# From the seventh query block on, the local scores and the preceding block's products with V become one task of the ordering list

## The chip, the cores and the metric

The kernel runs on one core of a Trainium2 chip. The metric is the device time of one launch in microseconds (us). Five engines work side by side, each through its own instructions in a fixed order: PE (TensorE, matmuls; its weight loads are listed as PEld), DVE (VectorE), ACT (ScalarE), POOL (GpSimd) and SP (SyncE, which here only issues DMAs). An engine that waits for a semaphore holds up everything behind it in its own list.

## The reference

The inputs q, k and v have 8 batches, 8 heads, 576 positions and 64 elements per head. The attention has two parts that are added; the result goes through a feed-forward network (FFN) with a residual.

```python
q_d = q.reshape(B, H, Sd, factor, D).mean(axis=3)      # factor 4: 144 pooled positions; k_d, v_d alike
out_up = np.repeat(sm_attn(q_d, k_d, v_d), factor, axis=2)
mask = np.abs(pos[:, None] - pos[None, :]) < factor     # a band of 7 positions
scores = np.where(mask, scale * q @ k.T, -1e9)
out_local = softmax(scores) @ v
x = (out_up + out_local)                                # 4608 tokens of 512
xn = (x - mean) / sqrt(var + 1e-6) * g_ln
out = x + relu(xn @ w_ch1) @ w_ch2                      # 512 -> 2048 -> 512
```

## The kernel before

**The FFN** fills most of PE's time. The 4608 tokens are 18 chunks of 256. For each chunk there are 8 pairs of hidden slices (2 x 128 of 2048 columns). An operand is split into a high and a low part, and each product is made of three matmuls (low by high, high by low, high by high). "Up" (`up`, L1048) makes `h` in PSUM, 12 matmuls of 128x256 for each slice; ACT makes `hh` from it (L1055) and DVE the rest `hl` (L1059); "down" (`down`, L1071) adds 6 matmuls of 128x512 for each slice into the two `acc` tiles of the chunk, which stay in PSUM for the chunk's whole life. The first two chunks run interleaved while the weights arrive. A weight slab `s` is loaded by two DMAs of SP, put together by ACT (L359) and DVE (L367, L370) as `cva`, and split by ACT (L378) and DVE (L383) into `hi` and `lo`. There are 32 slabs: `1_f` and `2_f` for f from 0 to 15.

**The local attention** has 40 query blocks (`local(i)`, i from 0 to 39, five for each batch, each of two rows of 58 queries against 64 keys). For the blocks from 7 on SP loads q and k in 128-byte pieces (`qr`, `kr`, L478, 16 DMAs for a block) and v (`vwin`, L496, 4 DMAs); DVE transposes q and k (`lqt`, `lkt`, L535); PE makes the scores `ls` with 32 matmuls of 64x64 (`scores_by_block`, L587); DVE adds the mask (L593), takes the largest (L598) and from block 12 on subtracts it (L603); ACT makes the exponentials `la` (L613; before block 12 eight small ones, L617, with a scaling on DVE, L600); PE transposes them (`lt`, L622); ACT copies them out (`at`, L629); PE multiplies them with V (`times_v`, `lv`, 32 matmuls of 64x65, L643); DVE takes inverses (`lr`, L649, L650) and divides (`xl`, L659; or ACT with four small instructions, L662); SP moves the rows to the token tiles (`x<-xl`, L708, L714). Two matmuls of 64x64 tiles stand in different quarters of the PE array and run at the same time, four of them side by side.

**The pooled attention** works on 16 half batches with two head pairs each: `raw` loads, POOL sums (L765, L766), PE transposes `gq` (L791), ACT copies (`qbdg`, L800, `ktg`, L804), PE scores `gs` (L818), DVE the largest `gmx` (L822), ACT exponentials `ag` (L831), PE transposes `gt` (L837), ACT `agt` (L847), PE products with V `gv` (L854), DVE `od`. Then each tile of 128 tokens is added up by POOL (L948), normed by DVE (`st`, `mv`, `xn`) and turned by PE (`px`, L975).

**What sets the order.** All of this is put on record as tasks of a list (`Plan.add`): an engine, an estimated duration, the tasks it depends on, a due time, and the rooms that it takes and gives back. Rooms are "u" (88 tiles of 2 KB in SBUF), "stg" (2 staging tiles) and "a" (the 8 PSUM tiles). `Plan.order` then pulls due times forward through the dependencies and puts one task after another: on the engine that can go on first, the ready task that is due first and whose rooms are free. The emitted instruction order of every engine is that order, and on the chip each engine follows it whatever the estimates were worth. A block's due time is `window_at(i)`: 25.2 units of the plan's own time from one block to the next, with blocks 5 and 6 put 50 units early. The scores of a block are due 6 units before it, its `lt` 3 before, its product with V 1 before. The loads of q and k are due 14 units before.

Of the kernel before, what the change touches and what calls it, by code (L numbers as in the profile page):

```python
# [22 lines left out]
class Plan:  # L23
# [14 lines left out]
    def add(self, eng, dur, fn, deps=(), due=0.0, take=(), give=(), lag=None, ahead=1e9, alt=None, kb=0):  # L38

        opts = {eng: (dur, fn, 0.0)}  # L40
        if alt is not None:
            opts[alt[0]] = alt[1:]
        t = SimpleNamespace(
            n=len(self.tasks), opts=opts, dur=dur, deps=[d for d in deps if d is not None],
            due=due, take=take, give=give, lag=lag, ahead=ahead, open=0.0, waits=0, eng=None, fn=None, kb=kb,
        )
        self.tasks.append(t)
        return t
# [91 lines left out]
def attention_then_ffn(  # L140
# [13 lines left out]
    B, H, S, D = q.shape  # L154
# [8 lines left out]
    NWIN = 5  # L163
# [7 lines left out]
    NPAIR = H // 2  # L171
    NU, NSTG = 88, 2
    NPE, NPB = 7, 1
    NVW = 4
# [2 lines left out]
    NU -= sum(SEP.values())  # L177
    SHIFTED = (0, 1, 2, 3)
    LATE = 12
    SCALE = 1.0 / float(D) ** 0.5  # L180
    POOLED_SCALE = SCALE / (FACTOR * FACTOR)
    out_f = out.rearrange("b s e -> (b s) e")
# [111 lines left out]
    def window_at(i):  # L294
        if NWIN <= i < NWIN + NEARLY:
            return w_base + i * w_gap - EARLY
        return w_base + i * w_gap if i >= NWIN else norm_at(0) - B0W - B0W_GAP * (2 - i)
# [7 lines left out]
    AHEAD = 45  # L305
# [4 lines left out]
    plan = Plan({"u": NU, "stg": NSTG, "a": 8, **SEP}, {"a": 2, "u": U_SPARE})  # L310
# [8 lines left out]
    U, A, STG = (("u", 1),), (("a", 1),), (("stg", 1),)  # L319
    DMA, LAT, W_AHEAD, W_LAG = 0.5, 2.5, 40, 1.5  # L320

    def act(n, sbuf=False):
        return (0.155 if sbuf else 0.14) + n / 1430.0

    def dve(n):
        return 0.06 + n / 950.0
# [132 lines left out]
    last_local = SimpleNamespace(v=[None] * NVW, ls=None)  # L459
# [3 lines left out]

    def local(i):
        b, w = divmod(i, NWIN)
        due = window_at(i)
        add = plan.add
        x = SimpleNamespace(r={}, p={}, raw={})
        vwin = vwins[i % NVW]
# [37 lines left out]
        turned = []  # L507
        by_pe = i < NPE
        own = b < NPB
        for src, nm in () if own else ((q, "q"), (k, "k")):  # L510
            if by_pe:
# [10 lines left out]
                def turn_out(nm=nm):  # L522
# [4 lines left out]
                t = add("SP", 1.33, lambda src=src, nm=nm: load_rows(src, nm), (), due - 12.0, take=U,  # L527
                        lag=LAT, kb=360, ahead=AHEAD)
                t = add("PE", 0.43, turn, (t,), due - 8.0, take=A, give=U)
# [15 lines left out]
        if own:  # L545
# [2 lines left out]
                if half in {int(window_start(w, par) + 64 > FACTOR * OWN_G[0][1]) for par in range(2)}:  # L548
                    turned += own_done[b, half]
            turned.append(last_local.ls)  # L550
        vt = add("SP", 2.65 if own else 2.65, load_v, (last_local.v[i % NVW],), due - 8.0, lag=LAT, kb=360, ahead=AHEAD)

        def scores_by_pair():

# [37 lines left out]
        def masked(n):  # L592
            nc.vector.tensor_add(x.ps[n], x.ps[n], mask.unsqueeze(1).broadcast_to([P, NPAIR, 64]))  # L593
# [37 lines left out]
        def times_v():  # L631


            x.pv = [
                psa(f"lv{i}_{n}")[:, : NPAIR * (D + 1)].rearrange("p (h e) -> p h e", h=NPAIR)
                for n in range(2)
            ]
            for pr in range(NPAIR):
                for n in range(2):
                    js = slice(64 * n, 64 * n + 64)  # L640
                    for m in range(2):
                        hs = slice(64 * m, 64 * m + 64)
                        nc.tensor.matmul(  # L643
                            x.pv[n][hs, pr], lhsT=x.at[js, pr, hs], rhs=vwin[js, m, pr], start=True, stop=True
                        )

        def inverse(h2):
            r = work.tile([P, NPAIR], F32, tag="lr", bufs=8, name=f"lr{i}_{h2}")
            nc.vector.tensor_scalar_add(r, x.pv[h2][:, :, D], 1e-9)  # L649
            nc.vector.reciprocal(r, r)  # L650
            x.r[h2] = r

        def divided(h2, eng):
# [7 lines left out]
            for pr in range(NPAIR):  # L661
                nc.scalar.activation(xl[:, pr], pv[:, pr, :D], AF.Copy, scale=r[:, pr : pr + 1])  # L662

        by_dve = i in SHIFTED or i >= LATE
        t = add("PE", 0.75, scores_by_pair if by_pe else scores_by_block, turned, due - 6.0,
                take=(("a", 2),), give=() if own and w not in (2, NWIN - 1) else (("u", 2 * NPAIR if own else 2),))
        if own:
            last_local.ls = t
        if not by_pe:
            t = add("DVE", dve(256), lambda: masked(0), (t,), due - 5.0)  # L670
            t = add("DVE", dve(256), lambda: masked(1), (t,), due - 5.0)
        t = add("DVE", 2 * dve(256) + (2 * dve(256) if by_dve else 0.15), largest_by_pair, (t,), due - 5.0)
        t = add("ACT", 2 * act(256) if by_dve else 1.6, exps_by_pair, (t,), due - 5.0, take=U, give=(("a", 2),))
        t = add("PE", 0.43, turn_a, (t,), due - 3.0, take=A, give=U)
        at = add("ACT", act(512), turn_a_out, (t,), due - 3.0, take=U, give=A)
        last_local.v[i % NVW] = tv = add("PE", 0.7, times_v, (at, vt), due - 1.0, take=(("a", 2),), give=U)
        outs = []
        for h2 in range(2):
            t = add("DVE", 0.28, lambda h2=h2: inverse(h2), (tv,), due)
# [5 lines left out]
        for par in range(2):  # L685
            s0 = NQ * (2 * w + par)
            n = min(NQ, S - s0)
            t, r0 = b * S + s0, s0 - window_start(w, par)
            while n:
                m = min(n, P - t % P)  # L690
                moves.append((t // P, t % P, r0, m, par))
                t, r0, n = t + m, r0 + m, n - m
# [478 lines left out]
```

## Time and profile before

| | |
|---|---|
| median of 3 runs | 1054.72 us (1051.92 to 1056.3) |
| profiled execution: its own time, which is its span | 1051.3 us |
| mean granted TensorE clock | 0.995 |
| PE busy | 1034.3 us, 98% |
| DVE / ACT / POOL busy | 514.0 / 309.8 / 251.0 us |
| 1152 + 1152 + 1152 matmuls of L1048, 3 x 576 of L1071 | busy 193.6 + 185.2 + 185.0 and 237.2 + 227.4 + 225.2 us, overlapping each other |
| `ls` by blocks, 1056 matmuls of 64x64 (L587) | busy 22.9 us |
| `lv`, 1280 matmuls of 64x65 (L643) | busy 28.2 us |

How to read it: matmuls are pipelined, so the records of one overlap those of the next, and what a group costs PE is read from the start of one record to the start of the next. In the timeline the first column is the start in us from the span's start, the second the time from the first start to the last end of the merged records; a bracket gives idle time just before and what ended it. In the windows, each engine has its busy time and the number of instructions, then come the granted PE clock (1.00 is full), the DMA share and GB/s.

### The profile page before, as it was taken

How to read it: one execution, taken by the hardware profiler on the slowest of the kernel's cores; microseconds unless marked ns; L12 is line 12 of the kernel's file. 1: busy time of each engine (PE TensorE's matmuls, PEld its weight loads, DVE VectorE, ACT ScalarE, POOL GpSimd, SP SyncE). 2: the span in 40 equal slices, each digit the busy share in tenths (PEclk: the TensorE clock that was granted, in tenths of full speed). 3: DMA queues.
4: the chain of work that ended last, by engine and by line, in shares of the span. 5: the costliest groups of instructions: out<-in, count | busy, mean ns of one | idle time of the engine just before them, and what ended most of it. 6: DMA issues, size and time to landing. Idle time of an engine off the chain costs nothing.

```text
span 1051.3 us, 24104 instructions
## 1 busy us (share of the span) xinstructions
PE 1034.3 (98%) x9450; PEld 928.9 (88%) x9450; DVE 514.0 (49%) x1301; ACT 309.8 (29%) x846; POOL 251.0 (24%) x272
## 2 busy tenths in 40 slices
PE   9999899999999999999999999999999999999998
PEld 8887798988899989989898989899989899888997
DVE  7799976343444435444434443544434444534211
ACT  6676533232212222221323222222221222221110
POOL 4213552214014320231404150141401300000000
PEclk9999999999999999999999999999999999999999
DMA  7897474434344534343434443253442443301000
GB/s 177 251 283 210 136 176 95 114 64 114 61 101 91 133 75 110 62 124 56 91 94 96 104 97 99 47 134 67 114 87 69 92 88 65 80 11 52 7 21 21
DMA packets 283702, 104.38 MB, mean 99 GB/s; under 512 B 229789, under 2 KB 270493, under 8 KB 283589
## 3 DMA queue, kind: packets, MB, share of 16 engines
q1 hardware_dynamic: 283589, 102.84, 40.8%
q8 instruction: 75, 1.23, 0.5%
q14 instruction: 38, 0.31, 0.1%
HBM read 82.58 MB, written 11.80 MB: 90 GB/s over the span
## 4 chain that ended last, share of the span: by engine, by line
PE 83%; DVE 6%; DMA 5%; SPq 2%; issue 1%; POOL 1%; ACT 1%; ACTq 0%; DVEq 0%; POOLq 0%
PE h L1048 34%; PE acc L1071 33%; PE gv L854 3%; DMA s<-in_moe_w_ch_dram 2%; PE gs L818 2%; PE lv L643 2%; PE ls L587 2%; DVE cva L370 2%; PE lt L622 1%; PE px L975 1%; PE gt L837 1%; DVE lo L383 1%; SPq L714 1%; DMA x<-xl 1%; DVE cva L367 1%
## 5 line engine op out<-in xcount | busy, mean ns | idle before, releaser
L1071 PE MATMUL acc<-hi,hl 128*128 128x512 f32 x576 | 237.2, 412 | 0.6 <-DVE hl L1059 0.5
L1071 PE MATMUL acc<-lo,hh 128*128 128x512 f32 x576 | 227.4, 395 | 0.0
L1071 PE MATMUL acc<-hi,hh 128*128 128x512 f32 x576 | 225.2, 391 | 0.0
L1059 DVE SCALAR_TENSOR_TENSOR hl<-h,hh 128x512 fp32r<-128x512 f32 x144 | 98.9, 687 | 250.7 <-ACT hh L1055 222.0
L1055 ACT ACTIVATE hh<-h 128x512 fp32r<-128x512 f32 x144 | 86.2, 599 | 430.3 <-PE h L1048 363.5
L1048 PE MATMUL h<-xh,lo 128*128 128x256 f32 x1152 | 193.6, 291 | 0.2 <-DVE lo L383 0.2
L1048 PE MATMUL h<-xh,hi 128*128 128x256 f32 x1152 | 185.2, 283 | 0.0
L1048 PE MATMUL h<-xlo,hi 128*128 128x256 f32 x1152 | 185.0, 283 | 0.0
L1048 PEld LDWEIGHTS h<-xh,lo 128*128 128x128 f32 x1152 | 169.0, 190 | 17.4 <-DVE lo L383 0.4
L1048 PEld LDWEIGHTS h<-xlo,hi 128*128 128x128 f32 x1152 | 158.9, 192 | 0.0
L1048 PEld LDWEIGHTS h<-xh,hi 128*128 128x128 f32 x1152 | 158.6, 191 | 0.0
L948 POOL TENSOR_TENSOR x<-x,up 128x512 f32<-128x512 f32 x32 | 41.2, 1287 | 386.3 <-DMA x<-xl 208.1
L1071 PEld LDWEIGHTS acc<-hi,hh 128*128 128x128 f32 x576 | 108.5, 188 | 25.0
L1071 PEld LDWEIGHTS acc<-hi,hl 128*128 128x128 f32 x576 | 109.2, 190 | 16.9 <-DVE hl L1059 1.2
L1071 PEld LDWEIGHTS acc<-lo,hh 128*128 128x128 f32 x576 | 109.5, 190 | 12.7 <-DVE lo L383 0.3
L982 ACT ACTIVATE xh<-px,gain 128x128 fp32r<-128x128 f32 x144 | 43.7, 372 | 72.7 <-PE px L975 42.4
L992 DVE SCALAR_TENSOR_TENSOR xlo<-px,gain,xh 128x128 fp32r<-128x128 f32 x144 | 43.1, 345 | 39.1 <-ACT xh L982 38.6
L1079 DVE SCALAR_TENSOR_TENSOR x<-acc,x 128x512 f32<-128x512 f32 x36 | 24.7, 689 | 39.8 <-PE acc L1071 39.8
L831 ACT ACTIVATE ag<-gs,gmx 96x144 f32<-96x144 f32 x96 | 29.0, 374 | 41.9 <-DVE gmx L823 34.4
L370 DVE SCALAR_TENSOR_TENSOR cva<-s,cva 128x256 int32<-128x256 int32 x64 | 40.0, 665 | 1.1
L854 PEld LDWEIGHTS gv<-vd,agt 72*72 72x72 f32 x512 | 37.1, 145 | 1.2
L854 PE MATMUL gv<-vd,agt 72*72 72x65 f32 x512 | 37.9, 228 | 0.0
(196 smaller groups left out, 1106.9 us busy)
## 6 DMA issues: line engine op xcount, KB each, us to landing
s<-in_moe_w_ch_dram SPq DMA_DIRECT2D x64, 256.0 KB
vwin<-in_v_dram SPq DMA_DIRECT2D x160, 64.0 KB
out_dram<-x SPq DMA_DIRECT2D x36, 256.0 KB
qr<-in_q_dram SPq DMA_DIRECT2D x264, 32.0 KB
kr<-in_k_dram SPq DMA_DIRECT2D x264, 32.0 KB
up<-ud SPq DMA_DIRECT2D x28, 256.0 KB
x<-xl SPq DMA_DIRECT2D x74, 42.0 KB
ud<-od SPq DMA_DIRECT2D x32, 72.0 KB
```

Source lines behind the costliest of these rows:

```text
L370: nc.vector.scalar_tensor_tensor(out=a, in0=x.raw[i].rearrange("p (n two) -> p n two", two=2)[:, :, 0], scalar=29, in1=a, op0=ALU.logical_ ...
L587: nc.tensor.matmul(x.ps[par][64 * h2 : 64 * h2 + 64, pr], lhsT=x.qt[hs, 2 * pr + h2], rhs=x.kt[hs, 2 * pr + h2], start=True, stop=True,)
L831: nc.scalar.activation(y.a[:, c], y.ps[:, c], AF.Exp, scale=POOLED_SCALE, bias=y.mx[:, c : c + 1])
L854: nc.tensor.matmul(y.pv[:, qh, h2], lhsT=y.at[kh][:, h2, qh * GH : (qh + 1) * GH], rhs=vd[:, kh, 2 * pr + h2], start=kh == 0, stop=kh == 1,)
L948: nc.gpsimd.tensor_add(xt[n], xt[n], x.up)
L982: nc.scalar.activation(xh[c][i][:, k, j * P : (j + 1) * P], pxt[n][:, kc], AF.Copy, scale=gain[:, kc : kc + 1])
L992: nc.vector.scalar_tensor_tensor(out=xlo[c][i][:, k, ts], in0=pxt[n][:, kc], scalar=gain[:, kc : kc + 1], in1=xh[c][i][:, k, ts].bitcast(F ...
L1048: nc.tensor.matmul(ph[c, p][:, fi], lhsT=wt[:, kc], rhs=xx[kc // 2][:, kc % 2], start=n == 0, stop=n == 3 * KC - 1)
L1055: nc.scalar.activation(hh[c, p], ph[c, p], AF.Relu)
L1059: nc.vector.scalar_tensor_tensor(out=hl[c, p].rearrange("p c t -> p (c t)"), in0=ph[c, p].rearrange("p c t -> p (c t)"), scalar=0.0, in1=h ...
L1071: nc.tensor.matmul(acc[c][j], lhsT=lt[:, fi, ts], rhs=rt, start=p == 0 and fi == 0 and n == 0, stop=p == NPR - 1 and fi == 1 and n == 2,)
L1079: nc.vector.scalar_tensor_tensor(out=x, in0=acc[c][j], scalar=1.0 + 2.0**-23, in1=x, op0=ALU.mult, op1=ALU.add)
```

## The change

`JOINED = 7`. For every block i from 7 on, the scores of block i are no longer a PE task of their own. They are emitted inside the task of block i-1's product with V: first `times_v` of i-1, then the scores of i, one task with an estimated duration of 1.25 (before: 0.7 and 0.75), the dependencies of both, four "a" rooms and the "u" rooms of both. There are 33 such joints (i from 7 to 39). Block 39's own product with V stays a task alone.

All that leads to the scores of block i takes its due time from `window_at(i - 1) + 5.0` in place of `window_at(i)`: the loads of q and k, their transposes, the scores, the mask, the exponentials, `lt` and `at`. The load of v, the product with V, the division and the moves keep `window_at(i)` (named `late`). The code from the inverses on is moved into a function `finish_local` and is unchanged in itself. The matmuls are the same in number and shape.

```diff
+    JOINED = 7
...
     def local(i):
         b, w = divmod(i, NWIN)
-        due = window_at(i)
+        late = window_at(i)
+        due = late if i < JOINED else window_at(i - 1) + 5.0
...
-        vt = add("SP", 2.65 if own else 2.65, load_v, (last_local.v[i % NVW],), due - 8.0, lag=LAT, kb=360, ahead=AHEAD)
+        vt = add("SP", 2.65, load_v, (last_local.v[i % NVW],), late - 8.0, lag=LAT, kb=360, ahead=AHEAD)
...
+        scores = scores_by_pair if by_pe else scores_by_block
+        done = 0 if own and w not in (2, NWIN - 1) else 2 * NPAIR if own else 2
+        if i < JOINED:
+            t = add("PE", 0.75, scores, turned, due - 6.0, take=(("a", 2),), give=(("u", done),) if done else ())
+        else:
+            t = last_local.join(scores, turned, done)
...
+        if i + 1 < JOINED or i == B * NWIN - 1:
+            last_local.v[i % NVW] = tv = add("PE", 0.7, times_v, (at, vt), late - 1.0, take=(("a", 2),), give=U)
+            finish_local(i, b, w, late, x, tv, own, by_pe)
+            return
+
+        def join(scores, turned, done):
+            def both():
+                times_v()
+                scores()
+
+            tv = add("PE", 1.25, both, [at, vt] + turned, late - 1.0, take=(("a", 4),), give=(("u", 1 + done),))
+            last_local.v[i % NVW] = tv
+            finish_local(i, b, w, late, x, tv, own, by_pe)
+            return tv
+
+        last_local.join = join
+
+    def finish_local(i, b, w, due, x, tv, own, by_pe):
```

Since a list of due times sets the order, the diff does not tell what moves. Three places show it. The first number in a tile's name is the block (`lv16`, `ls17`), the chunk (`h6`, `acc5`, `hl0`) or the matrix and slab (`lo1_5`, `cva2_4`); the last number is a buffer's. The lines of the changed file lie some lines further down than those of the profile.

PE, blocks 16 and 17, before: the product with V of block 16 stands between matmuls of the FFN, and so do the scores of block 17, further on.

```order
L1048 MATMUL h6_0_5704<-xlo6_1_5642,hi1_0_911 128x256 x2
L643 MATMUL lv16_0_5717<-vwin0_76,at16_5698 64x65 x2
L643 MATMUL lv16_1_5718<-vwin0_76,at16_5698 64x65 x2
...
L1048 MATMUL h6_0_5704<-xh6_0_5593,lo1_1_1155 128x256 x2
...
L837 MATMUL gt8_0_1_5879<-ident_66,ag8_0_5867 72x96 x3
L587 MATMUL ls17_0_5883<-lkt17_5586,lqt17_5408 64x64 x2
L587 MATMUL ls17_1_5884<-lkt17_5586,lqt17_5408 64x64 x2
...
L1071 MATMUL acc6_0_5842<-hi2_1_1284,hl6_0_5790 128x512
```

PE, the same blocks with the change (L645 is the product with V, L589 the scores, L1096 the FFN's "down").

```order
L1096 MATMUL acc5_1_5280<-hi2_10_2150,hh5_5_5572 128x512
L645 MATMUL lv16_0_5692<-vwin0_76,at16_5561 64x65 x2
L645 MATMUL lv16_1_5693<-vwin0_76,at16_5561 64x65 x2
...
L589 MATMUL ls17_0_5710<-lkt17_5367,lqt17_5365 64x64 x2
L589 MATMUL ls17_1_5711<-lkt17_5367,lqt17_5365 64x64 x2
...
L1096 MATMUL acc5_0_5279<-hi2_11_2165,hl5_5_5587 128x512
```

The 32 matmuls of `ls17` follow the 32 of `lv16` with nothing between them; before, eight FFN tasks and a `gs` and a `gt` lay between the two.

SP, in the stage in which the weights arrive, before: the weight slabs follow the last load of block 6.

```order
L487 DMA kn6_1075<-in_k_dram 64x8x64 x2
L352 DMA s2_4_0_1098<-in_moe_w_ch2_dram 128x512
L352 DMA s2_4_1_1099<-in_moe_w_ch2_dram 128x512
L352 DMA s2_5_0_1110<-in_moe_w_ch2_dram 128x512
L352 DMA s2_5_1_1111<-in_moe_w_ch2_dram 128x512
L502 DMA vwin2_78<-in_v_dram 64x4x64 x4
L347 DMA s1_6_0_1185<-in_moe_w_ch1_dram 128x2x256
```

SP at the same place with the change; where the line of dots stands, the rows of `qr7` and `kr7` come once more.

```order
L489 DMA kn6_1075<-in_k_dram 64x8x64 x2
L480 DMA qr7_1098<-in_q_dram 32x8x32 x4
L480 DMA kr7_1115<-in_k_dram 32x8x32 x4
L353 DMA s2_4_0_1166<-in_moe_w_ch2_dram 128x512
L353 DMA s2_4_1_1167<-in_moe_w_ch2_dram 128x512
...
L504 DMA vwin2_78<-in_v_dram 64x4x64 x4
L353 DMA s2_5_0_1310<-in_moe_w_ch2_dram 128x512
L353 DMA s2_5_1_1311<-in_moe_w_ch2_dram 128x512
L348 DMA s1_6_0_1346<-in_moe_w_ch1_dram 128x2x256
```

The 16 DMAs of block 7's q and k now stand ahead of the weight slabs from `s2_4` and `s2_5` on; before, they came after the slab `s2_14`.

DVE in the same stage, before.

```order
L383 TENSOR_TENSOR lo1_5_1540<-cva1_5_1232,hi1_5_1527 128x512
L367 TENSOR_SCALAR cva2_4_1347<-cva2_4_1347 128x512
...
L383 TENSOR_TENSOR lo2_4_1597<-cva2_4_1347,hi2_4_1575 128x512
L598 TENSOR_REDUCE lmx6_1614<-ls6_0_1577 128x4
L598 TENSOR_REDUCE lmx6_1614<-ls6_1_1578 128x4
```

DVE there with the change.

```order
L384 TENSOR_TENSOR lo1_5_1548<-cva1_5_1230,hi1_5_1522 128x512
L600 TENSOR_REDUCE lmx6_1556<-ls6_0_1528 128x4
...
L537 STREAM_TRANSPOSE lqt7_1569<-qr7_1098 128x512
L537 STREAM_TRANSPOSE lkt7_1593<-kr7_1115 128x512
L368 TENSOR_SCALAR cva2_4_1337<-cva2_4_1337 128x512
...
L384 TENSOR_TENSOR lo1_6_1737<-cva1_6_1442,hi1_6_1673 128x512
L595 TENSOR_TENSOR ls7_0_1712<-ls7_0_1712,mask_71 128x256
L687 TENSOR_SCALAR lr6_0_1748<-lv6_0_1687 128x4
```

Block 7's transposes, masks and maxima have moved in between the weight slabs; before, they came behind the slab `lo1_15`, when nearly all were done. Over the whole program DVE has 1196 rows in place of 1231 and ACT 655 in place of 620: the list now gives 39 halves of the division to ACT, before 4.

More of the change, by code (lines that the diff above doesn't have):

```diff
@@ L645, in times_v @@
                         )
+        by_dve = i in SHIFTED or i >= LATE
+        scores = scores_by_pair if by_pe else scores_by_block
[4 more added lines that the diff above has]
+            t = last_local.join(scores, turned, done)
+        if own:
+            last_local.ls = t
+        if not by_pe:
+            t = add("DVE", dve(256), lambda: masked(0), (t,), due - 5.0)
+            t = add("DVE", dve(256), lambda: masked(1), (t,), due - 5.0)
+        t = add("DVE", 2 * dve(256) + (2 * dve(256) if by_dve else 0.15), largest_by_pair, (t,), due - 5.0)
+        t = add("ACT", 2 * act(256) if by_dve else 1.6, exps_by_pair, (t,), due - 5.0, take=U, give=(("a", 2),))
+        t = add("PE", 0.43, turn_a, (t,), due - 3.0, take=A, give=U)
+        at = add("ACT", act(512), turn_a_out, (t,), due - 3.0, take=U, give=A)
+        if i + 1 < JOINED or i == B * NWIN - 1:
[12 more added lines that the diff above has]
+    def finish_local(i, b, w, due, x, tv, own, by_pe):
+        add = plan.add
         def inverse(h2):
@@ L662, in divided @@
                 nc.scalar.activation(xl[:, pr], pv[:, pr, :D], AF.Copy, scale=r[:, pr : pr + 1])
[L664 to L676, printed above, removed]
         outs = []
```

## Prediction

> **What bounds the kernel now.** I read the page first, then the windows, then PE's timeline.
>
> ```profile
> span 1051.3 us, 24104 instructions
> PE 1034.3 (98%) x9450; PEld 928.9 (88%) x9450; DVE 514.0 (49%) x1301; ACT 309.8 (29%) x846; POOL 251.0 (24%) x272
> PE 83%; DVE 6%; DMA 5%; SPq 2%; issue 1%; POOL 1%; ACT 1%; ACTq 0%; DVEq 0%; POOLq 0%
> ```
>
> PE has work for 98% of the span and makes 83% of the chain that ended last. The rest of the chain (DVE, DMA, SP's queue) lies in the start, as the windows show (first the stretch, then busy time of PE, PEld, DVE, ACT and POOL, then PEclk):
>
> ```profile
> 80.00:120.00 40.00, 36.39 (x296) 32.21 (x295) 39.28 (x75) 26.03 (x71) 19.65 (x16) 0.96 0.69 199
> 120.00:150.00 30.00, 27.48 (x201) 24.51 (x200) 25.38 (x47) 12.51 (x32) 12.68 (x13) 0.94 0.59 137
> 300.00:400.00 100.00, 100.00 (x909) 89.90 (x908) 45.38 (x121) 24.61 (x65) 31.43 (x32) 1.00 0.42 95
> ```
>
> From 80 to 120 us DVE is full (39.28 of 40) and PE idles 3.6 us; from 120 to 150 PE idles 2.5. From 300 on PE is never idle and DVE is at 45%. So there a saving counts only if it takes PE time away, and each PE us taken away shortens the span; in the start more DVE work can cost.
>
> **What a group of small matmuls costs PE.** A group of `lv` between "up" matmuls, and one of `ls` between "down" matmuls:
>
> ```profile
> 402.62 0.64 PE L1048 MATMUL h<-xh,hi 128*128 128x256 f32 x4
> 403.10 0.64 PE L1048 MATMUL h<-xlo,hi 128*128 128x256 f32 x4
> 403.67 0.70 PE L643 MATMUL lv<-vwin,at 64*64 64x65 f32 x32
> 404.30 0.74 PE L1048 MATMUL h<-xh,lo 128*128 128x256 f32 x4
> 404.88 0.64 PE L1048 MATMUL h<-xh,hi 128*128 128x256 f32 x4
> ...
> 367.88 0.39 PE L1071 MATMUL acc<-lo,hh 128*128 128x512 f32 x1
> 368.11 0.39 PE L1071 MATMUL acc<-hi,hh 128*128 128x512 f32 x1
> 368.43 0.69 PE L587 MATMUL ls<-lkt,lqt 64*64 64x64 f32 x32
> 369.05 0.50 PE L1071 MATMUL acc<-hi,hl 128*128 128x512 f32 x1
> 369.39 0.39 PE L1071 MATMUL acc<-lo,hh 128*128 128x512 f32 x1
> ```
>
> Go by starts. Four "up" matmuls take 0.48 (402.62 to 403.10). The four before `lv` take 0.57, `lv` itself 0.63, the four after it 0.58: inserting it costs 0.09 + 0.63 + 0.10 = 0.82 us. A "down" matmul takes 0.23; the one before `ls` takes 0.32, `ls` 0.62, the one after 0.34: again 0.09 + 0.62 + 0.11 = 0.82. Some of this is paid on going in and out, not for the 32 matmuls. How much, one place shows, where in the start two blocks' products with V stand one behind the other:
>
> ```profile
> 28.15 1.16 PE L643 MATMUL lv<-vwin,at 64*64 64x65 f32 x64
> ```
>
> 64 take 1.16 from first start to last end, 32 take 0.70: the second 32 add 0.46, where a group alone costs 0.82. Put behind another group, one costs 0.36 less; I take 0.35.
>
> **The change part by part.** *The joints.* 33 groups of `ls` move behind a group of `lv`: 33 x 0.35 = 11.6 us off PE, at places where PE is never idle. From both sides: the row of 64 is `lv` behind `lv`; `ls` behind `lv` has other operands and may keep one wait of PE's weight queue.
>
> ```profile
> L587 PEldq EVENT_SEMAPHORE  x14: 51/51/51, 180.6 to 933.8; - x14
> ```
>
> With 0.05 for it the joint saves 0.30 (9.9 us in all); above 0.36 (11.9) I see nothing. I take 11.6, since the nearest row is the same tile shape at the same place.
>
> *The early block 7.* Its due time falls by some 70 units, for block 6 is 50 units early itself. Its loads move ahead of the slabs from `s2_4` and `s2_5` on, its transposes, masks and maxima into the stage in which DVE is full.
>
> ```profile
> L478 SPq DMA_DIRECT2D qr<-in_q_dram x264: 311/449/1854, 136.1 to 899.1; - x132
> 0.00:80.00 80.00, 13.63 (x36) 1.00 0.87 237
> 0.00:80.00 80.00, 10.22 (x20) 1.00 0.87 237
> L535 DVE STREAM_TRANSPOSE lqt<-qr 128x512 f32<-128x512 f32 x33 | 23.3, 705 | 14.2 <-DMA kr<-in_k_dram 7.5 <-DMA x<-xl 2.6 <-DMA vwin<-in_v_dram 2.1
> L593 DVE TENSOR_TENSOR ls<-ls,mask 128x256 f32<-128x256 f32 x66 | 26.6, 424 | 23.0 <-PE ls L587 22.8
> L598 DVE TENSOR_REDUCE lmx<-ls 128x4 f32<-128x256 f32 x80 | 29.7, 412 | 0.6 <-PE ls L573 0.6
> L600 DVE TENSOR_SCALAR lmx<-lmx 128x8 f32<-128x8 f32 x8 | 3.3, 414 | 0.3
> ```
>
> On SP: 16 issues of 0.449 = 7.2 us, by which every slab behind them starts later. That is covered: the two windows to 80 us are of L359 (ACT, first step of a slab, two instructions each) and L370 (DVE, its next step). ACT has done 36, so 18 slabs have landed; DVE has done 20, so 10. Eight slabs wait for DVE, each for some 2 us of it: about 16 us of cover, against 7.2. On DVE: two transposes of 0.70, two masks of 0.42, two maxima and a scaling of 0.41 = 3.5 us more in a full stage (the division of block 7 stays where it was). PE waits for DVE there:
>
> ```profile
> 91.43 1.25 PE L643 MATMUL lv<-vwin,at 64*64 64x65 f32 x32 [2.19 <-ACT at L629]
> 130.79 1.06 PE L837 MATMUL gt<-ident,ag 96*72 96x96 f32 x6 [2.06 <-ACT ag L831]
> 91.00:95.00 4.00, 3.57 (x38) 2.98 (x39) 3.86 (x13) 3.12 (x10) 0.00 (x0) 0.57 0.70 177
> 224.00:228.00 4.00, 3.25 (x15) 3.24 (x16) 2.08 (x4) 1.71 (x7) 0.00 (x0) 0.57 0.44 102
> 784.00:788.00 4.00, 2.59 (x44) 2.00 (x43) 2.43 (x8) 3.15 (x12) 0.00 (x0) 1.00 0.86 157
> ```
>
> If every us that DVE is later becomes PE idle time, less the 0.8 that PE fills with block 7's own `ls` and `lt`, it costs 2.7; if the slabs that wait absorb it, 0. At the upper end a further price comes in: after waits of 2.19 the granted clock is 0.57 over four us, 4 x 0.43 = 1.7 us lost. So 0 to 4.4; I take 2.5, near the upper row, since DVE shows no slack there.
>
> The Trainium skill ("TensorE: Matmul & The Clock Gate", section "Part 1: The HAM clock gate") has the clock fall to half only after an idle window of about 3.4 us. By that page such a wait would cost itself alone and the upper end would be 2.7. The rows here show a fall after 2.19, so the rows decide.
>
> *The longer way from `ls` to `lt`.* After a joint, DVE has the inverses and a division of the block before among the masks and maxima of the next (0.65 to 1.1 us, by L649, L650 and L659), and `lt` waits for it. What covers it is the FFN work that stands between `ls` and `lt` on PE. Before, the least is 5.1 us, block 15:
>
> ```profile
> 373.18 0.67 ACT L613 ACTIVATE la<-ls 128x256 f32<-128x256 f32 x2
> 374.44 0.60 PE L622 MATMUL lt<-ident,la 128*128 128x128 f32 x4
> L649 DVE TENSOR_SCALAR lr<-lv 128x4 f32<-128x4 f32 x80 | 11.8, 147 | 35.9 <-PE lv L643 35.7
> L659 DVE TENSOR_TENSOR xl<-lv,lr 128x256 f32<-128x256 f32 x76 | 29.4, 407 | 0.3
> L662 ACT ACTIVATE xl<-lv,lr 128x64 f32<-128x64 f32 x16 | 3.6, 352 | 0.5 <-DVE lr L650 0.5
> ```
>
> `la` ends at 373.85, `lt` starts at 374.44: 0.59 to spare. In the new order the least is 5.2 us (three FFN tasks and a `gv`, four times). With 1.1 more on DVE these four wait 0.4 each. Nine of 28 `gs` now follow their `gq` after one FFN task, before five; each can wait for ACT. I put +1.5 for both; without any cover it would be 33 x 1.1 = 36.
>
> *The waits that PE has after the start.* They hang on chances of the order, which is now another:
>
> ```profile
> 222.96 0.94 PE L622 MATMUL lt<-ident,la 128*128 128x128 f32 x4 [1.25 <-ACT la L617]
> 224.75 1.75 PE L818 MATMUL gs<-ktg,qbdg 128*96 128x144 f32 x6 [0.85 <-ACT ktg L804]
> 786.60 0.98 PE L818 MATMUL gs<-ktg,qbdg 128*96 128x144 f32 x6 [1.41 <-DVE hl L1059]
> ```
>
> 1.25 + 0.85 + 1.41, and 1.7 for the clock at 224: 5.2 us. The first belongs to block 9, whose scores now come a block earlier, so it may go; others will come. I take -2, bounds -5.2 and 0.
>
> *At nothing:* the 35 halves of the division that go to ACT (four instructions of 0.35 for one of 0.41 on DVE; ACT is at 25% in the windows); `at` that is kept for most of a block's time in one of 88 tiles; the q and k loads a block earlier, as many as before. All lie beside PE's FFN work; a load that came late would hold up DVE's list and through `hl` PE.
>
> **The sum**, on the profiled execution: 1051.3 - 11.6 + 2.5 + 1.5 - 2.0 = 1041.7, that is -9.6. The median of the runs is 3.4 above that execution; I take the same difference from it: 1054.7 - 9.6 = 1045.
>
> **The rivals.** *The start takes most of it.* The DVE work of 3.5 comes through whole and two more waits each bring a slow clock, 3.5 + 2 x 1.7 = 6.9: -11.6 + 6.9 + 1.5 = -3.2, 1051.5. For it: DVE 39.28 of 40, and each wait of 2 us already there has its slow stretch. Against: the slabs have slack, and PE's list has other ready work. *The old waits vanish and no new ones come*: -11.6 - 5.2 = -16.8, 1038. For it: block 9's wait is tied to its place; against: one tight `gs` is as good as another. *Slower: PSUM runs short at the joints.* A joint takes four of the eight PSUM tiles at once and the two `acc` are always taken; two are left for `h` and for the small transposes, until DVE and ACT have read `lv` and `ls`. If the next "up" waits for that, it costs more than the joint saves from 0.35 us on; at 0.7 a joint: 33 x 0.7 = 23, -11.6 + 23 + 1.5 + 2.5 - 2 = +13, 1068. For it: DVE needs 3 us for what it reads there. Against: around the joints the new order puts "down" tasks, which take no new tile, as at blocks 16 and 17. *It doesn't do what it says:* PE empties between `lv` and `ls` all the same, as between other groups. Then 0 for the joints, 1051.3 + 2.0 = 1053.3, 1057 against the median. Against: the row of 64.
>
> The Trainium skill ("TensorEngine Tiling (Array Packing)", section "Tiling Modes") says that a change of the tiling mode drains the engine, and a change of tile alone does not. By that the last rival falls, since `lv` and `ls` are both in 64x64 mode; no run so far has `ls` behind `lv`.
>
> **How the numbers follow.** The forecast 0.62, with its own range 1041 to 1049; the start 0.16; the vanished waits 0.12; PSUM 0.05; nothing saved 0.05. The range 1038 to 1054 leaves out the two last, and the ends of the second and the third. A difference of 0.5% (5.3 us, so 1049.4 and 1060) is about what can be told from no change. Faster by more: 0.62 + 0.12 and a little of the start's, 0.76. Slower by more: PSUM, 0.05. The rest, 0.19, is within.
>
> **What would show it.** In the timeline after 300 us, `lv` x32 and `ls` x32 behind each other, from the start of the first to the start of the next FFN matmul 1.1 (0.63 + 0.46); 1.25 or more speaks for the last rival. The windows from 300 to 900 still have PE at 100 of 100. From 80 to 150 PE idles 6 to 9 us (before 6.1) with one or two stretches of clock under 0.9. L1048's idle time, now 0.2, stays under 1 us:
>
> ```profile
> L1048 PE MATMUL h<-xh,lo 128*128 128x256 f32 x1152 | 193.6, 291 | 0.2 <-DVE lo L383 0.2
> ```
>
> If it goes to 10 and more, PSUM ran short. I am wrong if the stage from 300 to 900 isn't about 8 us shorter for the same work, or if the start costs over 5.

## The result, and the profile after

The changed kernel takes 1067.13 us (median of 4 runs, 1063.38 to 1072.68). The kernel before took 1053.32 in runs beside them (4 runs, 1051.31 to 1056.3). The ratio is 1.0113, with a 95% interval from 1.0079 to 1.0148: slower by 1.1%, where 0.9% faster was forecast. The profiled execution is the slowest of the four, 1072.68 with a span of 1070.9; the profile before had a span of 1051.3. (A run's time is about 2 us more than its span.)

The head of the page after:

```profile
span 1070.9 us, 24256 instructions
PE 1038.8 (97%) x9464; PEld 939.4 (88%) x9464; DVE 500.1 (47%) x1266; ACT 340.2 (32%) x986; POOL 250.4 (23%) x272
```

PE's records add up to 4.5 us more than before (1034.3), though part of them was meant to take less. The reader should ask for the waits and for the clock.

**The joint does what was forecast.** The timeline of PE after, at the joint of blocks 16 and 17 (start, length, then the instruction):

```profile
485.21 0.70 PE L645 MATMUL lv<-vwin,at 64*64 64x65 f32 x32
485.72 0.65 PE L589 MATMUL ls<-lkt,lqt 64*64 64x64 f32 x32
486.30 0.74 PE L1073 MATMUL h<-xh,lo 128*128 128x256 f32 x4
```

From the first `lv` to the next "up" matmul it is 1.09 us, by 486.30 - 485.21. The forecast was 1.1. Over all 33 joints the median is 1.09. Two are longer: 1.40 at 210.5 us, and 3.28 at 94.5 us, where 14 filler matmuls (L198, put in where the list expects PE to idle) stand at its head. So some 0.36 us a joint, nearly 12 us, are taken off PE's work.

**Stages that were full no longer are.** The windows after (stretch, its length, busy time of PE, PEld, DVE, ACT and POOL with their counts, granted PE clock, DMA share, GB/s):

```profile
200.00:300.00 100.00, 94.70 (x867) 85.47 (x866) 39.06 (x105) 28.55 (x90) 27.25 (x28) 0.97 0.43 98
300.00:400.00 100.00, 100.00 (x925) 91.17 (x924) 45.57 (x117) 29.03 (x85) 29.53 (x30) 0.99 0.45 98
400.00:500.00 100.00, 95.36 (x874) 86.82 (x873) 43.52 (x115) 28.36 (x84) 21.44 (x23) 0.98 0.42 91
500.00:600.00 100.00, 97.56 (x846) 88.64 (x846) 40.97 (x104) 26.11 (x74) 25.44 (x26) 1.00 0.37 82
```

PE should have been at 100 of 100 in each of these from 300 on. From 200 us to the end, PE's gaps of over 0.12 us add up to 14.75 us; before, to 3.51. The waits of PE after, by instruction and releaser (total us, times, longest):

```profile
PE gt L862 <- ACT ag L856: 8.3, 2, 4.9
PE lt L624 <- ACT la L615: 6.7, 3, 3.1
PE gq L816 <- DVE hl L1084: 4.6, 1, 4.6
PE gv L879 <- DVE xl L697: 2.2, 1, 2.2
PE acc L1096 <- DVE hl L1084: 1.7, 1, 1.7
```

The first and the last row lie in the start, the other three after 200 us. Together these three are 13.5 of the 14.75 us.

**What `lt` waited for.** The timelines of SP, POOL, ACT and PE around the joint that starts at 283.9 us, the first of the three `la` waits:

```profile
270.31 6.71 SPq L739 DMA_DIRECT2D x<-xl  x8
...
290.96 8.87 SPq L739 DMA_DIRECT2D x<-xl  x10
...
294.81 1.26 POOL L973 TENSOR_TENSOR x<-x,up 128x512 f32<-128x512 f32 x1 [9.54 <-DMA x<-xl]
...
296.11 0.66 ACT L615 ACTIVATE la<-ls 128x256 f32<-128x256 f32 x2 [8.71 <-POOL x L973]
...
296.82 0.66 PE L624 MATMUL lt<-ident,la 128*128 128x128 f32 x4 [3.09 <-ACT la L615]
```

Read it from below. `lt` waits for the exponentials `la`. `la` does not wait for its scores; it waits for POOL's sum of a token tile, which gives back an SBUF tile that `la` is to be written to. The sum waits for the last 12 rows of its tile. They are the first two of the ten DMAs at 290.96; the second was issued at 291.86 and landed at 294.65. The rows had been ready since 286.94, when their division on DVE ended. SP came to them 4 us later, because it had been issuing one DMA after another, with no pause of over 0.5 us, since 265.05. In that stretch stand two moves of four DMAs, the row at 270.31: 6.71 us, where the list counts 1.8 for a move, so 3.6 for the two. (The 7.3 us for two such moves in the expectations of e5 and e7 is a misreading: the row it comes from, at 290.96, was shown only up to 298, and it begins with a move of two DMAs.) All issues of this line together (shortest, median and longest in ns):

```profile
L739 SPq DMA_DIRECT2D x<-xl x262: 597/811/1622, 201.6 to 993.6; - x131
```

A move is two or four of them, by how its rows can be cut. Of the 72 moves, 13 are of two and take 1.6 us by the median, 59 are of four and take 3.2. The list's 1.8 is right for the first kind and little over half of the second.

The waits of ACT and DVE show how this sits in the two kernels. Before:

```profile
DVE hl L1059 <- DMA x<-xl: 15.8, 3, 8.4
ACT hh L1055 <- DMA x<-xl: 14.5, 3, 6.0
```

After:

```profile
DVE st L981 <- POOL x L973: 45.7, 16, 7.1
ACT la L615 <- POOL x L973: 23.6, 3, 8.7
DVE hl L1084 <- POOL x L973: 17.7, 3, 8.5
```

Late moves were there before, too. They held up `hh` and `hl`, behind which PE had other FFN work. After, they hold up `la`, which has `lt`, the scores' PSUM tiles and the next joint behind it, and `st`, which stands at the head of DVE's list. The longest wait of PE after 200 us is of that second kind:

```profile
477.58 6.37 SPq L739 DMA_DIRECT2D x<-xl  x8
...
487.24 1.28 POOL L973 TENSOR_TENSOR x<-x,up 128x512 f32<-128x512 f32 x1 [11.84 <-DMA up<-ud]
488.55 0.69 DVE L981 BATCH_NORM_STATS2 st<-x 128x6 f32<-128x512 f32 x1 [5.15 <-POOL x L973]
...
491.80 0.69 DVE L1084 SCALAR_TENSOR_TENSOR hl<-h,hh 128x512 fp32r<-128x512 f32 x1 [2.15 <-DMA out_dram<-x]
492.41 0.42 DVE L595 TENSOR_TENSOR ls<-ls,mask 128x256 f32<-128x256 f32 x1
492.64 0.47 PE L816 MATMUL gq<-ident,qd 72*128 72x72 f32 x2 [4.64 <-DVE hl L1084]
```

The joint was at 485.21. DVE reads its scores for the first time at 492.41, since it stood at `st` and then at `hl`. All four PSUM tiles of the joint are unread until then, and `gq` finds no tile until `hl` has freed one. This sum waited not for rows but for `up`, whose load SP issued at 484.06, right behind the two moves of four at 477.58. `hl` then stood 2.15 us for the landing of a store of results.

The third kind of wait is the 2.2 us of `gv` at 217.67. There DVE's list stood at a transpose for a late load of q, which SP issued from 211.17 on, behind three moves that had taken it 7.3 us (from 201.63):

```profile
215.67 0.71 DVE L537 STREAM_TRANSPOSE lqt<-qr 128x512 f32<-128x512 f32 x1 [4.45 <-DMA qr<-in_q_dram]
```

**The start and the clock.** In the start DVE is full and the order of its list decides. The window from 138 to 147 us after:

```profile
138.00:147.00 9.00, 4.09 (x25) 3.30 (x23) 8.79 (x18) 3.20 (x8) 6.06 (x5) 0.85 0.43 118
```

PE does 4.09 of 9 us (before: 8.95). DVE works through weight slabs (L368, L371), and the maximum that `ag` needs comes behind them; `gt` waits 4.9 us for it. The waits from 80 to 200 us are 11.82 us, before 6.60.

One part of the difference is not the change's. The windows from 6 to 28 us, before and then after:

```profile
6.00:28.00 22.00, 21.17 (x456) 19.38 (x450) 15.42 (x40) 16.94 (x50) 9.11 (x16) 1.00 0.88 188
```

```profile
6.00:28.00 22.00, 22.00 (x302) 20.63 (x302) 9.52 (x22) 8.87 (x24) 10.61 (x17) 1.00 0.90 198
```

PE is busy all the time and gets through 302 matmuls in place of 456, though the first 1040 matmuls of PE's list are the same in both kernels. From the 80th to the 120th it takes 1.38 us before and 2.67 after, about half the speed. The first "up" begins 8.2 us later (62.9 against 54.6). The clock's record begins at 28.2 us in this execution and at 5.9 before, so the column shows 1.00 for what it did not record. The priced joint of the experiments (e7), whose list opens in the same way, has 445 matmuls in this window, and the profile of e4, which has no joint, shows the slow opening too; so the joints don't bring it. The profiled execution is 5.5 us above the median of its own kernel, and the opening is the likely reason.

The account of the two profiled executions:

| part | us |
|---|---|
| 33 joints of 0.36 | -11.9 |
| opening at a low clock, to the first "up" | +8.2 |
| PE's waits, 80 to 200 us (11.82 for 6.60) | +5.2 |
| PE's waits after 200 us (14.75 for 3.51) | +11.2 |
| stretches of half clock from 80 us on, less those at the end (20.5 us for 10.2, at half) | +5.1 |
| sum | +17.8 |
| difference of the spans | +19.6 |

1.8 us are left that I can't place. Without the opening the spans differ by 11.4 us; the medians differ by 13.8.

### The profile page after: what moved, and what is told of

Its sections match the earlier page's. It is cut to its first block, busy times and chain, and to the rows that moved or that the text cites. A ratio compares the mean times of both kernels' runs of the same rounds, so it can differ in the third digit from the quotient of the medians.

```text
span 1070.9 us, 24256 instructions
## 1 busy us (share of the span) xinstructions
PE 1038.8 (97%) x9464; PEld 939.4 (88%) x9464; DVE 500.1 (47%) x1266; ACT 340.2 (32%) x986; POOL 250.4 (23%) x272
## 5 line engine op out<-in xcount | busy, mean ns | idle before, releaser
L1096 PE MATMUL acc<-hi,hl 128*128 128x512 f32 x576 | 236.6, 411 | 1.7 <-DVE hl L1084 1.7
L1096 PE MATMUL acc<-lo,hh 128*128 128x512 f32 x576 | 228.1, 396 | 0.0
L1096 PE MATMUL acc<-hi,hh 128*128 128x512 f32 x576 | 226.5, 393 | 0.0
L1073 PE MATMUL h<-xh,lo 128*128 128x256 f32 x1152 | 193.8, 291 | 1.6 <-ACT xl L700 1.4
L1073 PE MATMUL h<-xh,hi 128*128 128x256 f32 x1152 | 186.1, 284 | 0.0
L1073 PEld LDWEIGHTS h<-xh,lo 128*128 128x128 f32 x1152 | 169.7, 191 | 18.2 <-ACT xl L700 1.8
L1073 PE MATMUL h<-xlo,hi 128*128 128x256 f32 x1152 | 185.4, 283 | 0.0
L1073 PEld LDWEIGHTS h<-xh,hi 128*128 128x128 f32 x1152 | 159.6, 192 | 0.0
L1073 PEld LDWEIGHTS h<-xlo,hi 128*128 128x128 f32 x1152 | 159.4, 192 | 0.0
L1096 PEld LDWEIGHTS acc<-hi,hh 128*128 128x128 f32 x576 | 109.0, 189 | 25.2
L1096 PEld LDWEIGHTS acc<-hi,hl 128*128 128x128 f32 x576 | 110.0, 191 | 16.7 <-DVE hl L1084 1.9
L1096 PEld LDWEIGHTS acc<-lo,hh 128*128 128x128 f32 x576 | 110.0, 191 | 13.1
L856 ACT ACTIVATE ag<-gs,gmx 96x144 f32<-96x144 f32 x96 | 29.1, 375 | 59.2 <-DVE gmx L848 54.6
L700 ACT ACTIVATE xl<-lv,lr 128x64 f32<-128x64 f32 x156 | 35.1, 333 | 29.5 <-DVE lr L688 17.7
L981 DVE BATCH_NORM_STATS2 st<-x 128x6 f32<-128x512 f32 x32 | 22.0, 688 | 45.7 <-POOL x L973 45.7
```

The costliest lines, as they stand in the source:

```text
L856: nc.scalar.activation(y.a[:, c], y.ps[:, c], AF.Exp, scale=POOLED_SCALE, bias=y.mx[:, c : c + 1])
L981: nc.vector.bn_stats(st, x.up if by_pe else xt[n])
L1073: nc.tensor.matmul(ph[c, p][:, fi], lhsT=wt[:, kc], rhs=xx[kc // 2][:, kc % 2], start=n == 0, stop=n == 3 * KC - 1)
L1096: nc.tensor.matmul(acc[c][j], lhsT=lt[:, fi, ts], rhs=rt, start=p == 0 and fi == 0 and n == 0, stop=p == NPR - 1 and fi == 1 and n == 2,)
```

## The experiments

All ratios are to runs of the kernel before that were taken beside them. "Waits" are PE's gaps of over 0.12 us after 200 us, in the last four fifths of the trace. The forecast expected few there, and none from 300 on.

| kernel | median us | ratio, 95% interval | waits |
|---|---|---|---|
| before | 1052.95 to 1056.56 in four sets of runs | 1 | 3.51 |
| the change | 1067.13 | 1.0113 (1.0079 to 1.0148) | 14.75 |
| e1: joined from block 12 | 1064.05 | 1.0069 (1.0038 to 1.0100) | 15.56 |
| e2: due times of the change, not joined | 1056.67 | 1.0034 (1.0009 to 1.0059) | 3.66 |
| e3: scores due 3 units later | 1065.94 | 1.0094 (1.0069 to 1.0120) | 15.35 |
| e4: before, blocks from 7 on 2 units earlier | 1050.73 | 0.9952 (0.9924 to 0.9979) | 1.71 |
| e5: joined, two DMAs for a move | 1047.59 | 0.9916 (0.9887 to 0.9945) | 1.12 |
| e6: before, two DMAs for a move | 1047.59 | 0.9919 (0.9890 to 0.9948) | 0.0 |
| e7: joined, a move priced at 3.6 | 1043.45 | 0.9879 (0.9854 to 0.9905) | 0.0 |
| e8: before with seven PSUM tiles | 1063.37 | 1.0073 (1.0044 to 1.0103) | 6.55 |
| e9: before, a move priced at 3.6 | 1048.14 | 0.9955 (0.9926 to 0.9984) | 1.32 |
| e10: e2 with a move priced at 3.6 | 1053.05 | 0.9984 (0.9956 to 1.0011) | 0.0 |
| e11: e1 with a move priced at 3.6 | 1040.06 | 0.9874 (0.9833 to 0.9915) | 0.7 |
| e12: joined from block 9, priced at 3.6 | 1038.83 | 0.9850 (0.9813 to 0.9887) | 0.49 |

### First: where the loss comes from

Three theories stood here: that the start takes it (START), that the joints themselves bring new waits (JOINT), or that any other order loses what the order before happened to have (ORDER).

**e1.** Only the blocks from 12 on are joined, so the start is that of the kernel before.

```diff
-    JOINED = 7
+    JOINED = 12
```

> Joints from block 12 on in place of 7 (28 joints); blocks 7 to 11 are due as in the kernel before. Three theories of why the changed kernel came out near 1067 us though each joint costs PE 1.09 us as forecast. START: block 7's work in the stage in which the weights arrive costs some 8 to 10 us there; then this run is near 1067 - 9 + 5 x 0.36 = 1060 or less, with PE idle between 80 and 150 us back near 6 us. JOINT: four PSUM tiles are taken at once, so that any delay of DVE or ACT after a joint reaches PE; then the waits of 2 to 5 us after 200 us stay (sum some 15 us) and the time is 1062 to 1067. ORDER: the order of before has unusually few waits and any newly drawn order has more, joints or not; then the waits after 200 us lie at other places, with a sum anywhere from 5 to 25 us.

1064.05, still slower than before. The waits from 80 to 200 us fall to 7.14, those after 200 stay at 15.56, as JOINT said. The start is a few us of the loss, not the bulk of it.

**e2.** The due times of the change stay, but each block's scores are a task of their own again.

```diff
-        if i < JOINED:
-            t = add("PE", 0.75, scores, turned, due - 6.0, take=(("a", 2),), give=(("u", done),) if done else ())
-        else:
-            t = last_local.join(scores, turned, done)
+        t = add("PE", 0.75, scores, turned, due - 6.0, take=(("a", 2),), give=(("u", done),) if done else ())
...
-        if i + 1 < JOINED or i == B * NWIN - 1:
+        if True:
```

> All due times of the change (q and k loads, scores, exponentials, lt and at of the blocks from 7 on a block earlier), but the scores are a task of their own again and take two PSUM tiles. No joint, so 11.6 us of PE time come back. JOINT: the waits after 200 us go with the joints; the time is then 1053 + what the start costs, 1055 to 1062. ORDER or a shortage of SBUF tiles through the earlier due times: the waits stay, and the time is 1067 + 11.6 less a little, 1072 to 1079. START: PE idle between 80 and 150 us stays near the changed kernel's 15 us.

1056.67, and 3.66 us of waits. The early due times alone don't bring the waits after 200 us. The joint adds 0.8% on top by the two ratios, that is 8.3 us (10.4 by the medians, which come from two sets of runs), where by its matmuls it should take off 11.9.

**e3.** The scores and all ahead of them are due 3 units later.

```diff
-        due = late if i < JOINED else window_at(i - 1) + 5.0
+        due = late if i < JOINED else window_at(i - 1) + 8.0
```

> The change with due times of window_at(i - 1) + 8.0 in place of + 5.0: the same joints, another draw of the order. JOINT: the sum of PE's waits after 200 us stays within 5 us of the changed kernel's, the time within 1063 to 1071. ORDER: the waits lie elsewhere and their sum differs by 5 us or more, to either side. START: no difference, block 7 is as early as before within 3 units.

1065.94 and 15.35 us of waits, at other places than with the change (the largest 3.6 for `lt`, 3.2 for `px`). In this kernel the divisions go mostly to DVE again, and the `lv` tiles are free after 3.3 us (mean of the last 28 blocks, from the first `lv` matmul to the end of the second division), against 5.2 with the change and 2.4 before. The waits are the same all the same. That spoke against PSUM held by `lv` as the cause.

**e4.** The kernel before, with the due times of the blocks from 7 on moved by 2 units, to have an order that was drawn anew.

```diff
-        due = window_at(i)
+        due = window_at(i) - (2.0 if i >= 7 else 0.0)
```

> The kernel before with the due times of the blocks from 7 on 2 units earlier: no joint, two PSUM tiles for each task, block 7 in its old stage, but another draw of the order. JOINT and START: 1052 to 1056, as before. ORDER: slower than before by 4 to 15 us, with waits of PE after 200 us that before did not have.

1050.73, rather a little faster. ORDER falls, as far as one more order can tell: another order as such costs nothing.

So the waits go with the joint, in three orders (14.75, 15.56, 15.35) and in none of the others. What in the joint makes them was open: its four PSUM tiles, or the late moves that the traces showed.

### Second: late moves or PSUM

**e5.** The changed kernel in the very order of the change on every engine, but with half the DMAs for a move.

```diff
-                for h2 in range(2):
-                    for r1, r2 in ((0, cut), (cut, m)) if cut else ((0, m),):
-                        nc.sync.dma_start(
-                            to[r1:r2].rearrange("p (c h d) -> p h c d", c=NPAIR, h=2)[:, h2],
-                            x.xl[64 * h2 + r0 + r1 : 64 * h2 + r0 + r2].rearrange("p (c n) d -> p n c d", n=2)[:, par],
-                        )
+                for r1, r2 in ((0, cut), (cut, m)) if cut else ((0, m),):
+                    nc.sync.dma_start(to[r1:r2], x.xl[r0 + r1 : r0 + r2].rearrange("p h d -> p (h d)"))
```

> The changed kernel, in the same order on every engine, but a move of rows to a token tile is issued as two DMAs of whole rows in place of four DMAs of 64-element pieces (what arrives in the token tiles is then not what belongs there; sizes and everything else stay). Theory MOVES: in the joined kernel x<-xl x8 takes SP 7.3 us (290.96) where the list counts 2 x 1.8, POOL's sum of the tile comes late, and with it the SBUF tile that the exponentials la of the next block wait for (8.71, 8.05, 6.81 us <-POOL x), behind which lt and the four PSUM tiles of the joint are held. Without these DMAs the PE waits after 200 us fall from 14.75 to 5 or less and the clock's drops go with them: about 1053. Theory PSUM: the joint takes four PSUM tiles at once and that alone brings the waits: they stay at 12 to 15 us, time 1064 to 1068.

1047.59, and the waits fall from 14.75 to 1.12, as MOVES said (its time, about 1053, was too high). No stretch of half clock is left between 200 us and the end. A move now takes SP 1.5 us by the median. Of the three kinds of wait only `gq`'s is left, with the order unchanged. The `la` rows of its waits:

```profile
ACT la L615 <- POOL x L969: 14.3, 3, 5.1
PEld lt L624 <- ACT la L615: 0.2, 1, 0.2
```

`la` still waits at the same three places, but 5.1 at most where it was 8.7, and `lt`'s cover of FFN work takes that up. The four tiles of a joint are the same as with the change, and `lv` holds its two for 5.0 us: PSUM taken by the joint is not enough to make PE wait.

**e6.** The control, the same edit on the kernel before.

> The kernel before with the same two DMAs in place of four for a move, as a control (what arrives in the token tiles is again not what belongs there). Theory MOVES: here the wait for late moves falls on hh and hl (6 to 8 us each, which PE hardly feels), so only 1 to 3 us are to be had: 1051 to 1054. Theory PSUM: nothing, 1053 to 1055.

1047.59 as well. Its waits after 200 us are gone (3.51 to 0), and its span is 5.3 us under that of the kernel before, by these waits and the clock's drop that went with them. That is more than the 1 to 3 us expected: cheap moves help both kernels. That e5 isn't ahead of e6 has its reason in the start: from 80 to 200 us it waits 13.71 us against 8.34, with 13.6 us of half clock against 3.4. That is 5.4 + 5.1 = 10.5 us, nearly what the joints save.

**e7.** The work is untouched; only the estimate is raised, to a little more than the 3.2 us that a move of four DMAs takes (it is now too high for those of two).

```diff
-            t = add("SP", 0.76 if by_pe else 1.8, move, outs, due + 1.0, take=() if n in piece else U,
+            t = add("SP", 0.76 if by_pe else 3.6, move, outs, due + 1.0, take=() if n in piece else U,
```

> The changed kernel with the list's estimate of a move of four DMAs raised from 1.8 to 3.6, as measured (7.3 us for two); the work is the same, the order is made again. Theory MOVES: the list now puts the exponentials and the sums where the tile is really free: waits after 200 us at 7 or less, 1053 to 1059. Theory PSUM: 12 to 15 us of waits as before, 1063 to 1068.

1043.45, faster than either theory said, and faster than the kernel before by 1.2%. The window from 200 to 1000 us:

```profile
200.00:1000.00 800.00, 800.00 (x7291) 727.34 (x7290) 345.33 (x906) 227.19 (x664) 181.64 (x186) 1.00 0.38 85
```

The same window with the change as it was:

```profile
200.00:1000.00 800.00, 785.17 (x7159) 712.04 (x7158) 340.37 (x893) 223.52 (x657) 182.75 (x187) 0.99 0.39 86
```

PE is at 800 of 800, and no `la` waits for POOL any more (what it waits for, in the row of its group):

```profile
L615 ACT ACTIVATE la<-ls 128x256 f32<-128x256 f32 x64 | 21.9, 390 | 9.8 <-DVE ls L605 8.1 <-issue 1.3
```

Its joints are as long as with the change (median 1.09), and `lv` holds its tiles for 4.6 us. e5 had made the transfers themselves coarser as well as SP's issues fewer; here both are as with the change, and only the order differs. What is left is the start:

```profile
PE gt L862 <- ACT ag L856: 8.2, 2, 4.6
```

**e8.** The kernel before with a PSUM tile less, in the list and on the chip.

```diff
-    plan = Plan({"u": NU, "stg": NSTG, "a": 8, **SEP}, {"a": 2, "u": U_SPARE})
+    plan = Plan({"u": NU, "stg": NSTG, "a": 7, **SEP}, {"a": 2, "u": U_SPARE})
...
-    ps_a = ctx.enter_context(tc.tile_pool(name="ps_a", bufs=8, space=bass.MemoryType.PSUM))
+    ps_a = ctx.enter_context(tc.tile_pool(name="ps_a", bufs=7, space=bass.MemoryType.PSUM))
```

> The kernel before with seven PSUM tiles in place of eight, in the list and on the chip; nothing joined. It prices a PSUM tile by itself. Theory PSUM: a joint holds on average less than one tile more than the two pieces apart (14 tile-us more in a block of 26 us), so a tile less all the time costs at least as much as the joint's waits, 10 us or more after 200 us: 1064 and above. Theory MOVES: PE waits stay under 6 us after 200 us, 1053 to 1058.

1063.37, slower by 0.7%, with 6.55 us of waits: neither the 10 of PSUM nor the under 6 of MOVES, and a time near PSUM's. A PSUM tile has a price, so theory MOVES was too simple where it gave PSUM none. But e5 and e7 have eight tiles and the joint's full use of them, and hardly any waits (1.12 and 0).

### Third: the joint by itself

**e9 and e10.** The edit of e7 on the kernel before, and on e2.

> The kernel before with only the estimate of a move raised from 1.8 to 3.6; nothing joined. It tells how much of the 13 us that the priced joint is under the kernel before is due to the price alone. Theory MOVES: the kernel before has 3.5 us of PE waits after 200 us and one or two drops of the clock to lose, so 1049 to 1053, and the joint is worth the rest, 7 to 10 us. Rival PRICE: the estimate is what was wrong in both, and the joint is worth little: then this kernel comes to 1043 to 1047 as well.

> The change's due times with the scores as a task of their own (not joined), and the estimate of a move at 3.6. Against the priced joint it has the joint alone taken away. If the joint saves 0.36 us each, 33 x 0.36 = 12, it comes to about 1055, with the start of the change (two or three waits of 2 to 5 us from 80 to 150). If the joint saves nothing on the path: 1043 to 1046.

e9: 1048.14, about 0.5% under the kernel before, 0.9 us below the range of MOVES and 1.1 above that of PRICE. e10: 1053.05, near the 1055 that a saving of 0.36 us a joint would give. So, by ratios: the price alone is worth 0.45%; the change's due times cost 0.29% on top (e9 to e10; by their medians, from runs side by side, 4.9 us); the joint then gives 1.05% (e10 to e7), that is 11 us, or 0.34 a joint. By the two intervals it can be 7 to 15 us. With the old price the same joint cost 8.3 us by ratios. The two edits can't be added up; each decides what the other is worth.

**e11 and e12.** Both keep the price and join from block 12, or from block 9 on.

> JOINED = 12 in place of 7, and the estimate of a move at 3.6. The start is that of the kernel before, and 28 joints in place of 33 are left. The priced joint from 7 on has 10.2 us of waits from 80 to 200 us and 13.6 us of half clock there (6.8 lost); the kernel before has 6.6 and one window of 3.4 (1.7 lost). If all of that goes with block 7: 8.7 saved less 5 x 0.36 = 1.8, about 1037. If the start is as it is whatever the block 7 does: 1045.

> JOINED = 9 and the estimate of a move at 3.6: blocks 7 and 8 have their scores behind the arrival of the weights as before, 31 joints are left. If the start's waits hang on block 7's work among the weight slabs: about 1036 (8.7 less 2 x 0.36). If they hang on anything that joins before 200 us (blocks 9 to 11): 1041 to 1044.

1040.06 for e11 and 1038.83 for e12. Each lies between the two times that its expectation gave. e12 has the lowest median of the study, 1.5% under the kernel before; its interval and e11's overlap. Its window from 80 to 200 us, and then that of e7:

```profile
80.00:200.00 120.00, 114.29 (x991) 102.06 (x990) 93.63 (x195) 56.89 (x160) 45.58 (x40) 0.99 0.56 147
```

```profile
80.00:200.00 120.00, 109.81 (x857) 98.70 (x856) 87.19 (x177) 55.65 (x162) 50.31 (x46) 0.94 0.61 160
```

Joining from 9 in place of 7 brings 3.1 us by the ratios (4.6 by the medians) and gives up two joints (0.7 us), so blocks 7 and 8, put early among the weight slabs, cost some 4 to 5 us. The intervals of e7 and e12 overlap, so this is a size and not a proof. It is less than the 8.7 that e12's expectation counted on: the waits from 80 to 200 us fall from 10.2 to 5.54, not to nothing.

All five orders that were made with a move at 3.6 (e7, e9 to e12) have 1.32 us of waits or less after 200 us, so e7's is no lucky draw.

## Why the prediction was wrong, point by point

- **The joints, -11.6.** Right. 1.09 us from `lv` to the next FFN matmul, and 11 us (7 to 15) by e10 to e7. "It doesn't do what it says" falls with it.
- **The longer way from `ls` to `lt`, +1.5. This is the step that failed.** It took DVE's 0.65 to 1.1 us of work in between as the only thing that could come late, and set it against 5.2 us of FFN work as cover. What came late was the SBUF tile that `la` is written to: 8.71, 8.05 and 6.81 us, through SP's list, in which moves of four DMAs take 3.2 us where 1.8 was counted, and POOL's sum. With what else was late behind SP's list, PE's waits after 200 us grew by 11.2 us and the half clock there by three stretches for one, 3.4 us: 14.6 in place of 1.5.
- **"At nothing".** The sentence looked at where the moved work lies and not at which room it waits for. It named a late load as the danger, by way of DVE's list and `hl`. That danger came about, at `gv` (2.21, a load of q) and by way of `hl` at `gq` (4.64, a load of `up` and a store), and what made the loads late were the moves ahead of them in SP's list: with cheap moves both waits shrink to 1.12 in all (e5). The row that held the warning was in the trace before: the DMAs of L714 take SP 0.81 us each by the median, four stand in 59 of the 72 moves, and the list counts 1.8 for a move.
- **The early block 7, +2.5 (0 to 4.4).** Too low. In the profiled execution the waits from 80 to 200 us grew by 5.2 and the half clock by 1.7, 6.9 in all; by e9 and e10 the early due times as a whole cost 3 to 4.9, by e7 and e12 blocks 7 and 8 cost some 4 to 5. The waits grew by more than the 3.5 us of added work, since `gt` stood behind weight slabs in DVE's list. The rival "The start takes most of it" had the place, and its 6.9 is met by chance: it counted 3.5 of work and two stretches of slow clock, where 5.2 of waits and one stretch were measured. What came after 200 us it left out.
- **The old waits, -2.** The waits of block 9's `lt` and of the two `gs` are gone, as the upper bound had them. New ones that the forecast counted above took their place.
- **The sum** was -9.6. With the terms as measured it is -11.9 + 14.6 + 6.9, and -5.2 for the old waits is already in these differences: +9.6. The medians differ by 13.8. Of the signs named ahead, the 1.1 us of a joint came true; a start that costs under 5 and PE at 100 of 100 from 300 to 900 did not (before, there was one gap in that stretch, the 1.41 at 786.6).
- **The rival "PSUM runs short at the joints"** had 0.05 and a time of 1068, and the median is 1067. That is luck, for its mechanism isn't the one at work. It charged each joint, at the "up" that follows. L1073's idle time went to 1.6 us, not to 10 (its group is below), and of the 31 joints after 200 us five have a wait of over 1 us within 18 us behind them. PSUM is the way on which a late `la` or `hl` reaches PE: the joint's four tiles are unread while ACT or DVE stand. That late moves alone don't do it shows in e2, that the joint's PSUM alone doesn't in e5. Whether a ninth tile would have hidden the late moves wasn't tried, since the kernel's pool has all eight.

```profile
L1073 PE MATMUL h<-xh,lo 128*128 128x256 f32 x1152 | 193.8, 291 | 1.6 <-ACT xl L700 1.4
```

The Trainium skill ("TensorEngine Tiling (Array Packing)", section "Tiling Modes") has the engine drain at a change of the tiling mode and not at a change of tile. On the second the trace agrees: both groups are in 64x64 mode, a pair takes 1.09 us, and there is no gap between `lv` and `ls`.

## What to carry to other kernels

Where a list of estimates sets the order, a wrong estimate costs little as long as what it makes late has cover (0.45% here, by e9). Before joining or moving tasks, compare the estimates of the queues that the order leans on with the durations in the trace (here SP's moves of four DMAs: 1.8 against 3.2), and follow not only what a moved instruction reads but whose tile it is written to, and who gives that tile back. A change that loses with one set of estimates may win with another: try the joint and the price apart and together before judging either.

## What the runs showed of the hardware

The opening at a low clock has no fixed length: the clock's record begins at 28.2 us in the profiled execution of the change, at 28.0 in that of e4, and between 4.7 and 7.1 in the other twelve. In the first it was worth 8.2 us, by the later first "up".

The length of a wait alone doesn't tell whether the clock falls. The windows behind a wait of 2.21 us (at 217.67) and behind one of 2.44 us (at 579.58), after:

```profile
217.00:223.00 6.00, 5.33 (x33) 4.87 (x34) 3.88 (x14) 3.17 (x13) 1.80 (x3) 0.72 0.79 183
579.00:585.00 6.00, 5.42 (x41) 5.16 (x42) 3.12 (x5) 1.24 (x4) 3.09 (x4) 1.00 0.17 35
```

The shorter one was followed by 3.4 us of half clock, the longer by none. The Trainium skill ("TensorE: Matmul & The Clock Gate", section "Part 1: The HAM clock gate") has the clock fall after at least one idle window of about 3.4 us, and has this window run freely, so that it doesn't reset when a kernel starts. The drop after 2.21 us disagrees with the first; that a longer wait went without one would fit the second, which no run here tests by itself.
